# Polysketch attention with a multiplicative feed-forward block: first queries transferred behind the first keys, and a new order of all steps

## The chip, the cores and the metric

The kernel runs on one core of a Trainium2 chip. Its engines run side by side, each through its own row of instructions: TensorE (PE, with its weight loads listed as PEld), VectorE (DVE), ScalarE (ACT), GpSimd (POOL) and SyncE (SP), which here only issues transfers. The metric is the device time of one execution in microseconds (us), a median of several.

## The reference

There are 4 batches of 4 heads, 1088 positions a head and 32 numbers a position. Both sketches have 8 rows, so that a position has 64 features.

```python
def phi(x):
    a = np.einsum('rd,bhsd->bhsr', S1, x)
    b = np.einsum('rd,bhsd->bhsr', S2, x)
    return np.einsum('bhsi,bhsj->bhsij', a, b).reshape(*x.shape[:-1], r * r)
q_p, k_p = phi(q), phi(k)
kv = np.einsum('bhsf,bhsd->bhfd', k_p, v)
z = np.sum(k_p, axis=2)
num = np.einsum('bhsf,bhfd->bhsd', q_p, kv)
den = np.einsum('bhsf,bhf->bhs', q_p, z)[..., None] + 1e-06
attn = (num / den).astype(np.float32)
x = attn.transpose(0, 2, 1, 3).reshape(B * S, H * D)      # 4352 x 128
a, b = x @ w1, x @ w2                                     # 4352 x 1024
return ((a * b @ w3) @ w_out).astype(np.float32)          # 4352 x 128
```

## The kernel before

**What is computed.** The product w3 @ w_out is formed once (steps `f0` to `f7`), so that the feed-forward block is (x @ w1) * (x @ w2) times one 1024x128 matrix. Its 4352 rows of x are cut into eight groups of 512, `g0` to `g7`, two for each batch, and one of 256, `gr`, for the last 64 positions of each head. A group has eight parts of 128 columns. Part 3 of group 1, for example, has the steps `g1.3a` (x @ w1, L1799), `g1.3c` (a copy out of PSUM, L1804), `g1.3b` (x @ w2, L1809), `g1.3m` (the product on DVE, L1815) and `g1.3o` (the product with the folded matrix, L1835). Groups 4 and 5, and 6 and 7, are done together in a scheme with fewer multiplications, `h4` and `h6` (function `seven`): its products use only 64 rows of TensorE each. Products named `a` use rows 0 to 63 and those named `b` use rows 64 to 127 (L1673; a step such as `h4.0a5` is product 5 of part 0 in the lower half, with the tile `xd`), so that two of them can run at once; the later products, `P1` to `P7` (L1759), use 64 of the 128 columns, again a lower and an upper half.

**How x comes about.** For each batch the keys' steps are `k0` to `k3`: the keys are split in a leading part and a rest (`lead`, `rest`, L211), TensorE sums their outer products (`gram`, L659), several small steps turn these sums into scale factors (`k0.N0`, `k0.Na`, `k0.Nb` at L936 and L937, `k0.Nf` at L949 on POOL, which makes the tile `RS`), and the features meet the values (`kv`). The queries' steps are `q0`, `q1`, ..., one for each group at first: their sketches (`A`, `C`; `q0.C1` at L1030 multiplies the queries by `RS`), features (`phi`, L1208), denominators, and at last x, transposed (`q0.xT0`, `q0.xT1`, L1291). The first matmul of the feed-forward block, `g0.4a`, needs that x and columns of w1, which are converted from the raw words (`w1.c0`, `w1.j0` at L466, `w1.a0` on POOL at L470).

**What sets the order.** Every step is a small function under its name. The kernel calls 1179 steps in the order of a table, `ORDER`, and then ties the instructions of each engine into one row in that order, so that no engine takes a later instruction of its row before an earlier one has been issued. Further tables say which engine runs a step (`POOL` for GpSimd instead of VectorE, `CPV` for copies on VectorE instead of ScalarE) and which buffer each allocation takes (`SLOTS`; the tag `x`, with three buffers, holds q, k by heads and v). A buffer taken again makes its new writer wait for the last reader of its old content.

**Transfers.** Nearly all loads are issued by SP; the first two halves of the keys (`k0.load0`, `k0.load1`) are issued by ACT. A bulk load on SP also waits until the bulk load four places earlier has landed (`UNDER_WAY = 4`):

```python
for ins, ahead in zip(bulk[UNDER_WAY:], bulk):
    tc.add_manual_dep(ins, ahead.name, landed, reason="under way")
```

**Fillers.** Twelve steps `warm0` to `warm11` multiply a tile of zeros (L255, 128x256 each) on TensorE at chosen places; `WARM` says how many matmuls each has, in all 53.

Of the kernel before, what the change touches and what calls it, by code (L numbers as in the profile page):

```python
# [41 lines left out]
    "raw": "010212120211221",
    "s": "012345671252360063202461521024214",
    "x": "012012201110",
# [21 lines left out]
    g0.0c g0.1c h4.1ac h4.1ad h6.1bc h6.2ad k0.kT1 k1.kvc k2.kT1 k2.kq k3.kT0 k3.kT1 k3.kq q0.xc0  # L66
    q0.xc1 q6.xT0 q6.xT2
# [8 lines left out]
c.zeros warm0 q0.load c.ident s.four c.act c.mask s.zero k0.zero v0.zero s.load k0.load0 k0.loadr q0.restT q0.tr  # L76
k0.load1 s.words kr0.load k0.tr1 s.pair s.low s.lead s.sum k0.max0 k0.max1 warm1 q0.max k0.tr0 warm2 kr0.tr kr0.kT
warm3 s.rest w1.load s.T s.P s.tc warm4 q0.l2 k0.kT1 s.Pc s.R k0.g k0.lead0 s.c s.blk k0.rest0 q1.tr k0.gram0 s.blkh
k1.zero s.Pm warm5 q0.l1 q0.A0 warm6 kr0.ab k0.lead1 q0.rm q0.sma q0.sta warm7 k0.kT0 v0.load v0.loadr k1.load k0.ab1
q0.sha k0.rest1 q0.C0 k0.gram1 k0.gram2 k0.gram3 k0.gram4 k0.ab0 k0.abc1 q1.max q0.C0t q0.sla q1.l2 k1.loadr s.Pp  # L80
k0.Gm k0.Gt k0.Ga w1.c1 k0.Gb k0.abc0 k0.T0 q1.l1 warm8 kr0.abc k0.kp1 q0.sca w1.j1 k0.Ta k0.kp0 k0.Gc w1.c0 k1.tr0
kr1.load k2.zero k1.tr1 k1.kT1 kr0.kp warm9 k0.N0 warm10 k0.Na warm11 k0.T1 k0.kv0 k0.Tc k0.Tb k0.N1 k0.Nb k0.Nh q1.rm
q0.al k0.Nf q0.phi0 q0.phi1 q0.A1 q0.smy w1.m1 k1.max q0.sty q0.shy k0.kv3 k0.kv1 k0.kv2 q0.sly s.KS k0.kvr kr1.tr
# [1851 lines left out]
```

## Time and profile before

| | |
|---|---|
| device time, median of 3 runs | 245.06 us (244.8 to 246.78) |
| profiled execution, span from first to last instruction | 244.1 us |
| profiled execution, its own time | not listed beside its span |
| TensorE busy | 236.2 us (97%) |
| VectorE busy | 206.7 us (85%) |
| GpSimd busy | 161.9 us (66%) |
| ScalarE busy | 123.5 us (51%) |
| chain that ended last | 87% TensorE, 5% DMA |
| granted TensorE clock | 9 or more tenths in all 40 slices |

"Busy" is the time in which at least one instruction of an engine runs. The chain that ended last is followed back from the last instruction, at each step to whatever released it. The median stands 0.96 us above the profiled span; what lies around the span (launch and end) is in that difference.

### The profile page before, as it was taken

The page shows a single profiled execution, that of the slowest core. Times are in us where ns is not written, and L with a number is a line of the kernel's source. Part 1 is how long each engine was busy: PE and PEld are TensorE (multiplying, and loading weights), DVE is VectorE, ACT ScalarE, POOL GpSimd, SP SyncE. Part 2 cuts the span into 40 slices and gives each one's busy share as a digit, 9 for nine tenths or more (in the row PEclk, how much of TensorE's full clock was granted, in tenths as well). Part 3 has the DMA queues.
Part 4 walks back from the last instruction along what each step waited for, and adds up shares of the span by engine and source line. Part 5 has one row for each costly group of instructions (what it writes and reads, how often), then busy time and mean ns, then how long its engine had stood idle before and what let it go on. Part 6 is the DMA issues. An engine that isn't in the chain of part 4 may idle for free.

```text
span 244.1 us, 6745 instructions
## 1 busy us (share of the span) xinstructions
PE 236.2 (97%) x2724; PEld 129.8 (53%) x2724; DVE 206.7 (85%) x421; ACT 123.5 (51%) x246; POOL 161.9 (66%) x203
## 2 busy tenths in 40 slices
PE   8998999899999999999999999999999999999994
PEld 5887454545545646766566444444443354463363
DVE  2876988999899998997899878498989789999792
ACT  3976957675666764593012914355651164730010
POOL 4576658344856998764583889929999425883670
PEclk9999999999999999999999999999999999999999
DMA  7959797078859897200000000360000000000054
GB/s 201 265 143 325 181 227 190 6 197 224 220 141 251 188 217 190 59 1 3 3 0 0 4 0 3 59 113 3 1 0 0 0 3 0 0 1 3 12 90 93
DMA packets 31935, 22.06 MB, mean 90 GB/s; under 512 B 21280, under 2 KB 26528, under 8 KB 31904
## 3 DMA queue, kind: packets, MB, share of 16 engines
q1 hardware_dynamic: 31360, 21.11, 35.1%
q8 instruction: 21, 0.34, 0.6%
q10 hardware_dynamic: 544, 0.52, 0.6%
q14 instruction: 10, 0.08, 0.1%
HBM read 19.40 MB, written 2.23 MB: 89 GB/s over the span
## 4 chain that ended last, share of the span: by engine, by line
PE 87%; DMA 5%; ACT 2%; POOL 2%; DVE 1%; issue 1%; POOLq 0%; SPq 0%
PE b_ps L1809 12%; PE ps_o L1835 12%; PE ps_X L1673 11%; PE a_ps L1799 11%; PE ps_o L1759 10%; PE ps_w3o L534 6%; PE ps_Y L1673 6%; PE ps_Z L1673 3%; PE ps_g L659 2%; PE ps_x L1527 2%; PE ps_ac L1374 2%; DMA qh<-in_q_dram 2%; DMA k<-in_k_dram 2%; PE ps_or L1824 2%; POOL ph L1208 1%; PE idle_ps L255 1%
## 5 line engine op out<-in xcount | busy, mean ns | idle before, releaser
L1673 PE MATMUL ps_X<-xd,wv 64*128 64x512 f32 x112 | 36.3, 593 | 0.0
L1799 PE MATMUL a_ps<-xT,w 128*128 128x512 f32 (+1 forms) x80 | 36.1, 562 | 0.0
L1809 PE MATMUL b_ps<-xT,w 128*128 128x512 f32 (+1 forms) x80 | 35.6, 555 | 0.0
L1804 ACT COPY ffa<-a_ps 128x512 f32<-128x512 f32 (+1 forms) x38 | 20.1, 540 | 29.2 <-PE a_ps L1799 26.7
L1707 POOL TENSOR_TENSOR hc<-hc 128x512 f32<-128x512 f32 x16 | 20.7, 1304 | 15.7 <-DVE hc L1685 15.5
L1835 PE MATMUL ps_o<-ab,w3o 128*128 128x512 f32 x64 | 29.6, 600 | 0.0
L1680 ACT COPY hc<-ps_X 128x512 f32<-128x512 f32 x38 | 21.3, 590 | 16.1 <-PE ps_X L1673 12.9
L1815 DVE TENSOR_TENSOR ab<-ffa,b_ps 128x512 f32<-128x512 f32 (+1 forms) x40 | 23.9, 623 | 4.9 <-PE b_ps L1809 4.1
L501 POOL TENSOR_TENSOR w3c<-w3c,cv_m 128x512 int32<-128x512 int32 x16 | 21.2, 1344 | 4.2 <-DVE w3c L495 4.1
L1673 PEld LDWEIGHTS ps_X<-xd,wv 64*128 64x128 f32 x112 | 14.9, 186 | 13.1 <-issue 10.9
L1799 PEld LDWEIGHTS a_ps<-xT,w 128*128 128x128 f32 x80 | 14.1, 189 | 13.9 <-issue 8.8
L1809 PEld LDWEIGHTS b_ps<-xT,w 128*128 128x128 f32 x80 | 14.4, 190 | 13.1 <-issue 8.1
L1673 PE MATMUL ps_Y<-xd,wv 64*128 64x512 f32 x48 | 19.7, 594 | 0.0
L1835 PEld LDWEIGHTS ps_o<-ab,w3o 128*128 128x128 f32 x64 | 11.6, 190 | 13.4 <-issue 13.0
L534 PEld LDWEIGHTS ps_w3o<-wo,w3T 128*128 128x128 f32 x128 | 15.3, 192 | 2.4 <-issue 2.4
L534 PE MATMUL ps_w3o<-wo,w3T 128*128 128x128 f32 x128 | 15.7, 276 | 0.0
L1759 PE MATMUL ps_o<-hc,w3o 128*64 128x512 f32 x32 | 15.1, 595 | 0.0
L1759 PE MATMUL ps_o<-tt,ws 128*64 128x512 f32 x32 | 13.7, 594 | 0.0
L1680 ACT COPY hc<-ps_Y 128x512 f32<-128x512 f32 x14 | 8.1, 592 | 9.7 <-PE ps_Y L1673 6.6
L263 ACT ACTIVATE cv_c<-raw 128x1024 f32<-128x1024 f32 (+1 forms) x13 | 13.0, 1014 | 0.0
L1540 ACT COPY xd<-ps_x 64x256 f32<-64x256 f32 x24 | 8.8, 367 | 7.2 <-PE ps_o L1835 6.8
L1497 POOL COPY nz<-nz 32x8 f32<-32x8 f32 x32 | 11.1, 347 | 1.4
(347 smaller groups left out, 593.0 us busy)
## 6 DMA issues: line engine op xcount, KB each, us to landing
raw<-in_moe_w_dram SPq DMA_DIRECT2D x32, 256.0 KB, 5.0
qh<-in_q_dram SPq DMA_DIRECT2D x4, 544.0 KB, 4.5
raw<-in_moe_w_dram SPq DMA_DIRECT2D x4, 512.0 KB, 5.8
out_dram<-oT SPq DMA_DIRECT2D x32, 64.0 KB, 2.0
k<-in_k_dram SPq DMA_DIRECT2D x3, 512.0 KB, 5.1
v<-in_v_dram SPq DMA_DIRECT2D x2, 512.0 KB, 6.1
kh<-in_k_dram SPq DMA_DIRECT2D x8, 128.0 KB, 3.6
raw<-in_moe_w_out_dram SPq DMA_DIRECT2D x4, 256.0 KB, 5.0
```

Of the source, the lines that this page charges most:

```text
L263: act.activation(dst, hi.bitcast(F32), ACT.Prelu, scale=2.0 ** -112, alpha=-2.0 ** 32)
L501: pool.tensor_tensor(d, d, x["m"][:, i * 512:(i + 1) * 512], ALU.add)
L534: pe.matmul(t["o"], w3T[ko][:, c], wo[:, c], start=c == 0, stop=c == NC - 1)
L1673: pe.matmul(x[bank], stat(j, u)[:, i * 128:(i + 1) * 128], rows(j, u), start=new, stop=True, tile_position=(u * 64, 0), skip_group_check=True)
L1680: cp(n(y))(x[k], x[bank])
L1707: on(f"h{g}.{i}m{k}").tensor_mul(both[0][k], both[0][k], both[1][k])
L1759: pe.matmul(acc_o[bank][half[0]:half[1]], w(i), x(i), start=n == 1, stop=n == (2 if j == 3 else 4), tile_position=(0, half[0]), skip_group ...
L1799: pe.matmul(x["a"][:, :w], w_of(0, c), xT[g][:, c0:c0 + w], start=True, stop=True)
L1804: cp(f"g{g}.{c}{su}c")(x["s"][:, :w], x["a"][:, :w])
L1809: pe.matmul(x["b"][:, :w], w_of(1, c), xT[g][:, c0:c0 + w], start=True, stop=True)
L1815: dve.tensor_mul(ab_sb[g, c][:, c0:c0 + w], x["s"][:, :w], x["b"][:, :w])
L1835: pe.matmul(o_ps[g], w3o[:, c], ab_sb[g, c], start=n == 1, stop=n == NC)
```

## The change

Only tables change: `ORDER`, `SLOTS`, `POOL` and `CPV`. The set of steps is the same, and so is each step's arithmetic. In the order of loads on SP, the first queries (`q0.load`) move behind the sketch matrices and the last keys of batch 0, and the values of batch 0 and the keys by heads of batch 2 (`kh2.load`) trade places with other loads. The dummy activation `c.act` moves from the start to the end. 36 steps go from GpSimd to VectorE, 40 from VectorE to GpSimd, 7 copies from VectorE to ScalarE and 19 copies from ScalarE to VectorE. Lines of the diff, long tables cut:

```diff
 SLOTS = {
...
-    "x": "012012201110",
+    "x": "012011210102",
 }
...
 POOL = set("""
-    g4.oS g5.oS g6.oS g7.oS h4.0T1 h4.0T2 h4.0T3 h4.0m12 h4.0m22 h4.1T2 h4.1m11 h4.1m12 h4.2m11
+    g4.oS g6.oS h4.0T1 h4.0T2 h4.0T3 h4.0T4 h4.0m11 h4.0m12 h4.0m22 h4.1T1 h4.1T3 h4.1m11 h4.1m22
...
 CPV = set("""
-    g0.0c g0.1c h4.1ac h4.1ad h6.1bc h6.2ad k0.kT1 k1.kvc k2.kT1 k2.kq k3.kT0 k3.kT1 k3.kq q0.xc0
-    q0.xc1 q6.xT0 q6.xT2
+    g0.1c g1.3c g2.0c g2.1c g2.4c g3.6c h4.0ac h4.0bc h4.0bd h4.1ac h4.1be h4.2ac h4.2ad h4.k1
+    h6.0ac h6.0ae h6.1ac h6.3ae h6.3ai h6.3be k0.kT1 k2.kq k3.kq q0.xc0 q4.xT1 q6.xT0
...
 ORDER = """
-c.zeros warm0 q0.load c.ident s.four c.act c.mask s.zero k0.zero v0.zero s.load k0.load0 k0.loadr q0.restT q0.tr
...
-g1.oT g2.6o h4.1a5 g3.oT h4.0b5 h4.0bd h4.0a1 h4.0ac g2.oT h4.s3 h4.0b1 o.S2 h4.0bc h4.1a1 h4.1ac h4.1b1 h4.0b2 h4.0a2
+c.ident k0.zero k0.load0 c.zeros s.load k0.load1 s.words warm2 c.mask k0.loadr s.pair warm0 k0.tr0 s.low warm5 s.zero
...
+qr.phi0 v.4 g1.4o warm8 q6.pT1 q6.x q6.xT2 q6.xT3 g3.6o g0.oT g3.4o qr.pT0 g1.oT g2.oT h4.s1 qr.x q6.xT0 h4.0b1 q6.xT1
+h4.0a1 g3.oT h4.0a5 g0.st h6.s1 qr.xT0 h4.1b1 h4.s2 h4.0a2 h4.0b5 h4.s4 h4.s3 h4.0ac h4.0bc h4.0a6 h4.1a1 h4.0ah
...
 """
```

On SP, the first loads before, from the start of its row (`qh` are the queries of batch 0, `s_raw` the sketch matrices, `kr` the last keys, `raw` words of a weight matrix, here w1):

```order
L975 DMA qh<-in_q_dram 128x1088
L287 DMA s_raw<-in_S_dram 8x32 x2
L572 DMA k<-in_k_dram 64x4x32
L609 DMA kr_161<-in_k_dram 64x4x32 x2
L430 DMA raw<-in_moe_w_dram 128x512 x2
L582 DMA v<-in_v_dram 128x4x256
L593 DMA v<-in_v_dram 64x4x32
L560 DMA k<-in_k_dram 128x4x256
```

And now (`kh` are the keys of batch 2 by heads, in four pieces):

```order
L287 DMA s_raw<-in_S_dram 8x32 x2
L572 DMA k<-in_k_dram 64x4x32
L975 DMA qh<-in_q_dram 128x1088
L609 DMA kr_189<-in_k_dram 64x4x32 x2
L609 DMA kr_198<-in_k_dram 64x4x32 x2
L430 DMA raw<-in_moe_w_dram 128x512 x2
L572 DMA k<-in_k_dram 64x4x32
L560 DMA k<-in_k_dram 128x4x256
L593 DMA v<-in_v_dram 64x4x32
L582 DMA v<-in_v_dram 128x4x256
L601 DMA kh<-in_k_dram 32x1024 x4
```

The queries now stand behind three small loads. The values of batch 0 (`v`) stand behind the keys of batch 1, and take the buffer in which the queries of batch 0 were; `kh` has come forward, right behind them.

On DVE, the rows ahead of and with the first x before, from the sum `s_loy` of the step `q0.sly` on:

```order
L1101 TENSOR_TENSOR s_loy<-s_loy,ay_C_601 128x128
L1180 TENSOR_TENSOR s_pr<-s_al,s_loy 128x128
L1184 TENSOR_TENSOR s_pr<-s_pr 128x128
L1189 TENSOR_REDUCE s_d<-s_pr 128x2x16
L1194 SCALAR_TENSOR_TENSOR s_rc<-s_d 128x16
L1198 RECIPROCAL s_rc<-s_rc 128x16
L466 TENSOR_SCALAR w_81<-cv_c 128x2x256
L1274 COPY xc<-ps_xt 128x256 x2
L1291 TENSOR_TENSOR xT<-xc,ps_xs 128x256 x2
```

And now, between the same two steps (`s_hl`, `s_t_589` and `ay_C` of 128x384 belong to the queries of group 1, `kT` to the keys of batch 2):

```order
L1101 TENSOR_TENSOR s_loy<-s_loy,ay_C_574 128x128
L204 SCALAR_TENSOR_TENSOR s_hl<-s_g,s_t_589 128x2x128
L1157 TENSOR_TENSOR s_hl<-ps_a,s_hl 128x2x128
L1130 STREAM_TRANSPOSE ay_C<-ps_c 128x384
L1189 TENSOR_REDUCE s_d<-s_pr 128x2x16
L1194 SCALAR_TENSOR_TENSOR s_rc<-s_d 128x16
L1198 RECIPROCAL s_rc<-s_rc 128x16
L466 TENSOR_SCALAR w_81<-cv_c 128x2x256
L720 STREAM_TRANSPOSE kT<-kh 128x512
L1274 COPY xc<-ps_xt 128x256
L1291 TENSOR_TENSOR xT<-xc,ps_xs 128x256 x2
```

Two small products have gone to GpSimd and one copy to ScalarE; three steps of group 1 and the transposition of `kh` have come in between.

On TensorE, near the middle of its row, between the eighth-part products of the groups 0 to 3 (`ps_o`) and the products that make x of later groups (`ps_x`), there stands before:

```order
L534 MATMUL ps_w3o<-wo,w3T 128x128 x8
L1835 MATMUL ps_o<-ab,w3o 128x512
L1527 MATMUL ps_x<-pT,kq_2311 32x256 x32
L1835 MATMUL ps_o<-ab,w3o 128x512 x12
L1527 MATMUL ps_x<-pT,kq_2079 32x256 x32
```

And now:

```order
L1527 MATMUL ps_x<-pT,kq_2286 32x256 x32
L1835 MATMUL ps_o<-ab,w3o 128x512 x6
L255 LDWEIGHTS zeros
L255 MATMUL idle_ps<-zeros 128x256
L255 LDWEIGHTS zeros
L255 MATMUL idle_ps<-zeros 128x256
L1835 MATMUL ps_o<-ab,w3o 128x512
L255 LDWEIGHTS zeros
L255 MATMUL idle_ps<-zeros 128x256
L1527 MATMUL ps_x<-pT,kq_2328 32x256 x32
```

Three fillers (`warm7` and `warm8`) stand there now. Six more (`warm6`, `warm9`, `warm10`, `warm11`) have come from the start to places between these and the first feed-forward matmul.

163 lines of the change are left out of this document (81 added, 82 removed).

## The prediction

> **What bounds the kernel now.** I read the page's totals first, then the engines' busy time by stretches, with cuts at the first feed-forward matmul, at the ends of the regions without idle time, and at TensorE's last matmul.
>
> ```profile
> span 244.1 us, 6745 instructions
> PE 236.2 (97%) x2724; PEld 129.8 (53%) x2724; DVE 206.7 (85%) x421; ACT 123.5 (51%) x246; POOL 161.9 (66%) x203
> PE 87%; DMA 5%; ACT 2%; POOL 2%; DVE 1%; issue 1%; POOLq 0%; SPq 0%
> ```
>
> ```profile
> core 0: us, PE busy (x) PEld busy (x) DVE busy (x) ACT busy (x) POOL busy (x), PEclk, DMA share, GB/s
> 0.00:27.42 27.42, 24.49 (x506) 19.60 (x507) 18.01 (x58) 19.16 (x46) 15.23 (x52) 1.00 0.76 222
> 27.42:60.00 32.58, 31.18 (x625) 16.64 (x626) 29.44 (x81) 22.72 (x41) 17.94 (x24) 1.00 0.69 174
> 60.00:130.00 70.00, 70.00 (x941) 41.74 (x941) 63.71 (x124) 36.78 (x66) 52.19 (x42) 1.00 0.46 114
> 130.00:155.70 25.70, 25.70 (x255) 12.22 (x253) 20.19 (x39) 11.78 (x31) 19.60 (x20) 1.00 0.01 2
> 155.70:195.40 39.70, 39.70 (x185) 16.88 (x184) 34.25 (x55) 17.68 (x32) 30.78 (x34) 1.00 0.16 27
> 195.40:240.56 45.16, 45.16 (x218) 22.75 (x218) 40.86 (x67) 15.35 (x31) 26.18 (x35) 1.00 0.13 21
> 240.56:244.10 3.54, 0.00 (x0) 0.00 (x0) 0.29 (x1) 0.00 (x0) 0.00 (x0) 0.87 0.33 74
> ```
>
> TensorE is the bound from 27.42 to 240.56: from 60 on it is busy all the time, and 27.42 to 60 has 32.58 - 31.18 = 1.40 us without it. So an engine that gets faster or slower there changes nothing until TensorE waits for it. The change can move three things: when the feed-forward matmuls begin, how much TensorE has to do after that, and where it waits. Before 27.42 TensorE is busy too, but much of that is fillers; there the end of a chain decides, which I followed back from the first feed-forward matmul:
>
> ```profile
> 7.67 0.19 ACT L207 ACTIVATION_READ_ACCUMULATOR k_abs<-k 128x1 f32 x1
> 10.25 0.82 ACT L211 ACTIVATE kk<-k,k_g 128x640 f32<-128x640 f32 x1
> 18.96 0.16 DVE L937 TENSOR_TENSOR RC<-RC,ps_Nr 128x8 f32<-128x8 f32 x1 [0.41 <-PE ps_Nr L912]
> 19.20 0.67 POOL L949 TENSOR_TENSOR RS<-RC,mask 128x64 f32<-128x64 f32 x1
> 22.52 0.40 PE L1030 MATMUL ps_cy<-q,RS 128*32 128x128 f32 x8
> 23.20 0.32 DVE L1068 STREAM_TRANSPOSE ay_C<-ps_cy 128x128 f32<-128x128 f32 x1 [1.38 <-PE ps_cy L1030]
> 26.48 0.79 DVE L1291 TENSOR_TENSOR xT<-xc,ps_xs 128x256 f32<-128x256 f32 x2
> 27.42 1.96 PE L1799 MATMUL a_ps<-xT,w 128*128 128x512 f32 x4
> ```
>
> The keys' maxima are there at 7.67 + 0.19 = 7.86, but the second half's leading part (`k0.lead1`, ACT) starts only at 10.25, behind steps of the queries. From there sums and scale factors lead to 18.96 + 0.16 = 19.12 (`k0.Nb`), and from that 8.30 us lead to the first matmul: `RS` on POOL, `q0.C1`, for which DVE idles 1.38, and then DVE without a pause.
>
> **The start, part one: the keys' chain.** With the queries behind the first keys, `k0.lead1` stands on ACT directly behind the maxima. It can start some 10.25 - 7.86 = 2.4 us earlier; other small copies ahead of it take back a part. I take 2.1, as an estimate, for everything up to `k0.Nb`. The lower end is 0.5: the same 16 DMA engines carry everything (0.76 busy up to 27.42), and queries that land later may hold up what then stands behind them. The upper end is 3.5, if the keys land earlier too. Nine fillers (two each of `warm10`, `warm11` and `warm7`, one each of `warm6`, `warm8` and `warm9`) leave the first 18 us. Their price is the pitch of a run of them:
>
> ```profile
> 16.99 0.27 PE L255 MATMUL idle_ps<-zeros 128*128 128x256 bf16 x1
> 17.36 0.61 PE L255 MATMUL idle_ps<-zeros 128*128 128x256 bf16 x4
> ```
>
> (0.61 - 0.27) / 3 = 0.11 us each, 1.0 for nine. Ahead of the first feed-forward matmul they mostly filled waits; I credit the chain with half, 0.5.
>
> **The start, part two: DVE from `k0.Nb` to the first x.** Here the new row of DVE holds more. Added are `k0.kp1` (from POOL), `q0.al`, five steps of group 1 (`q1.sm`, `q1.st`, `q1.sh`, `q1.sl`, `q1.Ct`) and `k2.kT0`; two products and a copy go. The prices:
>
> ```profile
> L677 DVE TENSOR_TENSOR kp<-kab 128x1024 f32<-128x1024 f32 x1 | 1.2, 1206 | 0.0
> L720 DVE STREAM_TRANSPOSE kT<-kh 128x512 f32<-128x512 f32 x4 | 2.8, 704 | 0.3 <-POOL s_bs L1204 0.3
> L1137 DVE TENSOR_REDUCE s_g<-ps_a 128x32 f32<-128x256 f32 x1 | 0.4, 416 | 0.0
> L201 DVE SCALAR_TENSOR_TENSOR s_t<-s_g,ps_a 128x256 f32<-128x256 f32 x1 | 0.4, 420 | 0.0
> L204 DVE SCALAR_TENSOR_TENSOR s_hl<-s_g,s_t 128x256 f32<-128x256 f32 x3 | 1.3, 419 | 0.1
> L1157 DVE TENSOR_TENSOR s_hl<-ps_a,s_hl 128x256 f32<-128x256 f32 x1 | 0.4, 424 | 0.0
> L1130 DVE STREAM_TRANSPOSE ay_C<-ps_c 128x384 f32<-128x384 f32 x1 | 0.6, 575 | 0.0
> L1180 DVE TENSOR_TENSOR s_pr<-s_al,s_loy 128x128 f32<-128x128 f32 x1 | 0.3, 294 | 0.0
> L1274 DVE COPY xc<-ps_xt 128x256 f32<-128x256 f32 x2 | 0.7, 412 | 0.0
> ```
>
> 1.21 for `kp1`, 0.70 for `kT0`, 0.42 + 0.42 + 0.42 + 0.42 + 0.58 = 2.26 for group 1, and 0.28 for `al`, an estimate from the 128x128 product, add up to 4.45; away go `q0.p2` and `q0.p12` (0.29 each, the second of the same shape) and one copy (0.41): 1.0. That is 3.4 us more on DVE (one of two equal halves of `phi` comes and the other leaves). Against it stands the 1.38 of idle time, which the added work fills, since `kp1` needs nothing that comes late. The two products on POOL cost 0.3 more in handing over, an estimate from the gap of 0.08 before `RS` on each of four handovers. The start comes to -2.1 - 0.5 + 3.4 - 1.4 + 0.3 = **-0.3**, that is the first feed-forward matmul at about 27.1. Its range goes from -2.4 (all the new work in waits) to +2.5 (below).
>
> **TensorE after the start.** The useful work is the same. The nine fillers now stand where TensorE has no idle time: **+1.0**, and 0 if each falls into a wait.
>
> The products of `h4` and `h6` use half of the array, and two that use different halves run together:
>
> ```profile
> 156.67 0.59 PE L1673 MATMUL ps_X<-xd,w 64*128 64x512 f32 x1
> 156.68 0.59 PE L1673 MATMUL ps_X<-xd,wv 64*128 64x512 f32 x1
> 157.10 0.59 PE L1673 MATMUL ps_X<-xd,w 64*128 64x512 f32 x1
> 157.11 0.59 PE L1673 MATMUL ps_X<-xd,wv 64*128 64x512 f32 x1
> ```
>
> Each pass of a pair takes 157.10 - 156.67 = 0.43 us, and each product has two passes, so one that runs alone wastes 0.86 / 2 = 0.43. Of the 168 products, lower and upper ones alternated in pairs before. Now the order is `h4.0b1`, `h4.0a1`, `h4.0a5`, `h4.1b1`, `h4.0a2`, `h4.0b5`, and so on: between two instructions that use the whole array, I count 45 of one half and 44 of the other, then 25 and 26, then 14 and 14. Where TensorE lets a product of the free half go ahead, only the two odd ones run alone: **+0.9**, or 1.7 where its look-ahead is two products. It does go out of order elsewhere in the trace: the sums of the keys alternate two operands (`kk` and `k,kk`) head by head in the program, and still
>
> ```profile
> 9.50 0.33 PE L659 MATMUL ps_g<-kk 128*32 128x64 f32 x7
> 9.61 0.19 PE L659 MATMUL ps_g<-k,kk 128*32 128x32 f32 x1
> ```
>
> seven of one kind started ahead of the first of the other. [...]
>
> **Stalls from 27.42 to 60.** The largest piece of the 1.40 is
>
> ```profile
> 45.83 1.16 issue
> ```
>
> in the middle of the keys of batch 2 (the chain between 44 and 48 us). `k2.gram` now comes earlier among more matmuls of group 0, since the `kh` of batch 2 has come forward. I take half of the 1.40, **-0.7**; all of it may go (-1.4), and new waits of the same size may come (+1.2).
>
> POOL receives 24 us of DVE work and gives up 45 us; both engines stay below TensorE in every stretch after 60, where DVE has 70.00 - 63.71 = 6.3 us to spare and POOL 18. The copies moved between ACT and DVE are covered likewise; their cover is that TensorE has other parts' matmuls to do, and if it is gone the cost is a stall of one copy, about 0.6 us. The dummy activation at the end costs nothing: ACT is idle in the last stretch. The last 3.54 us are unchanged.
>
> **The sum.** Against the span of 244.1: -0.3 + 1.0 + 0.9 - 0.7 = +0.9, so 245.0. The median of the runs, 245.06, stands 0.96 above that span, which I take to be what lies around it: 245.0 + 0.96 = 246.0 us.
>
> **The rivals.** One per cent, about what a measurement of this kernel can tell from no change, lies at 242.6 and 247.5.
>
> *A, strict order of the halves.* If products start only in the order of the program, two neighbours of the same half cannot run together. Counting the order that way leaves 20 products alone: 20 x 0.43 = 8.6 instead of 0.9, or 246.0 + 7.7 = 253.7. For it speaks nothing in the rows, against it 9.50 and 9.61. 7%.
>
> *B, the late transfer.* The values of batch 0 now take the queries' buffer, so their load waits for `q0.restT` on DVE, which now stands behind the first sum of the keys; and the fourth piece of `kh` waits until those values have landed. `k2.kT0` needs all four pieces and stands on DVE ahead of the first x.
>
> ```profile
> v<-in_v_dram SPq DMA_DIRECT2D x2, 512.0 KB, 6.1
> kh<-in_k_dram SPq DMA_DIRECT2D x8, 128.0 KB, 3.6
> ```
>
> ```profile
> 14.91 0.19 DVE L217 TENSOR_REDUCE G_g<-ps_g 128x1 f32<-128x32 f32 x1 [1.35 <-PE ps_g L659]
> ```
>
> With `q0.restT` at about 13 (an estimate: the sum of `gram4` is taken up at 14.9 before, less 2.1), the last piece lands at 13 + 6.1 + 3.6 = 22.7, some 2 us ahead of DVE, which comes to it at about 25. If these loads take 2 us longer than that, for want of bandwidth, DVE stands still with all of group 0 behind it. At 4.5 us longer the first matmul is 2.5 late instead of 0.3 early: 246.0 + 2.8 = 248.8, slower. It decides from a landing of `kh` after 25 on. 16%.
>
> *C, the start gains in full.* The work added on DVE lies in waits, the first matmul comes 2.4 earlier (2.1 more than I took), the stalls go entirely (0.7 more) and the fillers stand in waits (1.0 less): 246.0 - 3.8 = 242.2, faster. For it speaks that most of the added DVE steps belong to group 1 and have to be done soon after anyway; against it that DVE had one pause only, of 1.38. 20%.
>
> *D, no gain on the keys' chain.* The loads share their engines, so the maxima or the sums come later by about 1.1 than I took: 247.1, within 1%. The change would then not do what its order of loads says. 10%.
>
> **How the numbers follow.** The forecast, 246.0, has the remaining 47%; D is within 1% as well: 0.57. Faster is C, 0.20. Slower are A and B, 0.23. The range runs from 242.0, just below C, to 249.0, just above B; outside lie A and the tails of B and C, less than 2 in 10. Each unknown's bounds alone stay in it: the start -2.4 to +2.5 gives 243.9 to 248.8, the stalls 245.3 to 247.9, the halves 246.0 to 246.8.
>
> **What would show it.** In the profile of the changed kernel: the first row of L1799 at about 27.1 (24.9 for C, 29.9 for B, with a wait of DVE at L720 released by the transfer `kh`); `k0.Nb` at about 17.0; passes of L1673 still in pairs 0.43 apart in the stretch of `h4` (single passes 0.43 apart there for A); nine fillers at L255 after the first L1799; less than 1.4 us without TensorE between its first L1799 and 60. It would be wrong as a whole if TensorE were idle for more than 2 us anywhere after 60: then a move of work between DVE, POOL and ACT, which I cost at nothing, would be the bound.

## The result and the profile after

The changed kernel takes 252.86 us (median of 4 runs, 252.56 to 254.27), beside 245.92 (244.8 to 246.78) for the kernel before: a ratio of 1.031, 95% interval 1.026 to 1.037. It is slower; 246.0 was forecast. Here and below a median is over all executions of a kernel, while ratios and intervals leave out those more than 1.5% above its fastest. The profiled span went from 244.1 to 250.8 us.

The page of the changed kernel, its totals, its chain by engine and its clock:

```profile
span 250.8 us, 6757 instructions
PE 243.6 (97%) x2724; PEld 143.2 (57%) x2724; DVE 216.3 (86%) x429; ACT 116.7 (47%) x234; POOL 147.0 (59%) x207
PE 86%; DVE 8%; DMA 2%; SPq 2%; issue 1%; ACT 0%; DVEq 0%
PEclk9957999999999999999999999999999999999999
```

TensorE has the same 2724 matmuls and is busy 243.6 - 236.2 = 7.4 us longer with them. In the third and fourth slice of the clock row (12.5 to 25 us) it ran at 0.5 and 0.7. The busy times by stretches, with cuts at the same events as before (first feed-forward matmul, first product of `h4`, TensorE's last matmul):

```profile
core 0: us, PE busy (x) PEld busy (x) DVE busy (x) ACT busy (x) POOL busy (x), PEclk, DMA share, GB/s
0.00:30.86 30.86, 27.69 (x497) 22.93 (x498) 19.63 (x63) 20.78 (x47) 16.17 (x54) 0.83 0.70 205
30.86:60.00 29.14, 29.04 (x606) 15.45 (x606) 28.45 (x72) 22.63 (x40) 11.10 (x20) 1.00 0.85 217
...
158.20:199.20 41.00, 41.00 (x184) 22.21 (x178) 35.90 (x57) 14.86 (x33) 31.31 (x34) 1.00 0.08 14
199.20:246.84 47.64, 47.63 (x224) 27.78 (x222) 42.86 (x72) 14.41 (x30) 25.91 (x43) 1.00 0.11 18
246.84:250.80 3.96, 0.00 (x1) 0.00 (x0) 0.11 (x1) 0.27 (x1) 0.00 (x0) 0.96 0.39 83
```

After the start TensorE is idle for 29.14 - 29.04 = 0.10 us and then never, and still the last two working stretches take 88.64 us where they took 84.85. The accounts, from the cuts of the two traces:

| stretch | before | after | difference |
|---|---|---|---|
| start to first feed-forward matmul | 27.42 | 30.86 | +3.44 |
| from there to the first product of `h4` | 128.29 | 127.34 | -0.95 |
| from there to TensorE's last matmul | 84.85 | 88.64 | +3.79 |
| tail | 3.54 | 3.96 | +0.42 |
| span | 244.1 | 250.8 | +6.7 |

So two places lose, the start and the products on half of the array. The start of the changed kernel, in order of time (start, length, then the wait before in brackets):

```profile
8.25 0.30 PE L819 MATMUL ps_krt<-ident,kr 128*128 128x128 f32 x1 [0.49 <-DMA kr<-in_k_dram]
11.01 0.30 PE L819 MATMUL ps_krt<-ident,kr 128*128 128x128 f32 x1 [0.72 <-DMA kr<-in_k_dram]
13.01 0.19 DVE L217 TENSOR_REDUCE G_g<-ps_g 128x1 f32<-128x32 f32 x1 [1.35 <-PE ps_g L659]
21.30 0.16 DVE L937 TENSOR_TENSOR RC<-RC,ps_Nr 128x8 f32<-128x8 f32 x1
29.03 0.70 DVE L720 STREAM_TRANSPOSE kT<-kh 128x512 f32<-128x512 f32 x1
30.86 1.10 PE L1799 MATMUL a_ps<-xT,w 128*128 128x512 f32 x2 [0.31 <-DVE xT L1291]
```

`k0.Gm` is taken up at 13.01 instead of 14.91, 1.90 earlier, as the order of loads promised. But `k0.Nb` ends at 21.30 + 0.16 = 21.46 instead of 19.12, 2.34 later, so that 8.45 us lie between the two where 4.21 did. From there to the first matmul it is 9.40 instead of 8.30, +1.10. The two rows of TensorE (`kr0.tr`, `kr1.tr`) wait for the last keys of batch 0; fillers stood about there before.

### The profile page after: what moved, and what is told of

Its sections match the earlier page's. It is cut to its first block, busy times and chain, and to the rows that moved or that the text cites. A ratio compares the mean times of both kernels' runs of the same rounds, so it can differ in the third digit from the quotient of the medians.

```text
span 250.8 us, 6757 instructions
## 1 busy us (share of the span) xinstructions
PE 243.6 (97%) x2724; PEld 143.2 (57%) x2724; DVE 216.3 (86%) x429; ACT 116.7 (47%) x234; POOL 147.0 (59%) x207
## 4 chain that ended last, share of the span: by engine, by line
PE 86%; DVE 8%; DMA 2%; SPq 2%; issue 1%; ACT 0%; DVEq 0%
PE ps_X L1673 12%; PE b_ps L1809 12%; PE ps_o L1835 11%; PE a_ps L1799 11%; PE ps_o L1759 10%; PE ps_Y L1673 6%; PE ps_w3o L534 6%; PE ps_Z L1673 3%; DMA kr<-in_k_dram 2%; PE ps_x L1527 2%; PE ps_ac L1374 2%; PE ps_g L659 2%; PE ps_or L1824 2%; PE ps_ab L702 1%; PE ps_kv L769 1%; DVE kk L651 1%
## 5 line engine op out<-in xcount | busy, mean ns | idle before, releaser
L1673 PE MATMUL ps_X<-xd,wv 64*128 64x512 f32 x112 | 41.4, 596 | 0.0
L1804 ACT COPY ffa<-a_ps 128x512 f32<-128x512 f32 (+1 forms) x34 | 17.4, 534 | 40.6 <-PE a_ps L1799 38.0
L501 POOL TENSOR_TENSOR w3c<-w3c,cv_m 128x512 int32<-128x512 int32 x16 | 22.2, 1404 | 6.1 <-DVE w3c L495 6.0
L1680 ACT COPY hc<-ps_X 128x512 f32<-128x512 f32 x29 | 15.9, 591 | 16.2 <-PE ps_X L1673 11.1
L1673 PEld LDWEIGHTS ps_X<-xd,wv 64*128 64x128 f32 x112 | 17.6, 186 | 9.2 <-issue 5.8
L1809 PEld LDWEIGHTS b_ps<-xT,w 128*128 128x128 f32 x80 | 14.3, 190 | 12.5 <-issue 9.0
L1673 PE MATMUL ps_Y<-xd,wv 64*128 64x512 f32 x48 | 21.1, 596 | 0.0
L1707 POOL TENSOR_TENSOR hc<-hc 128x512 f32<-128x512 f32 x14 | 17.7, 1269 | 2.5 <-DVE hc L1685 2.4
L1540 ACT COPY xd<-ps_x 64x256 f32<-64x256 f32 x24 | 8.8, 366 | 13.6 <-PE ps_x L1527 13.2
L1759 PE MATMUL ps_o<-hc,ws 128*64 128x512 f32 x32 | 14.6, 594 | 0.0
L538 ACT COPY w3o<-ps_w3o 128x128 f32<-128x128 f32 x8 | 2.1, 267 | 20.9 <-PE ps_w3o L534 20.9
```

The lines of the kernel that those rows point to most:

```text
L501: pool.tensor_tensor(d, d, x["m"][:, i * 512:(i + 1) * 512], ALU.add)
L1673: pe.matmul(x[bank], stat(j, u)[:, i * 128:(i + 1) * 128], rows(j, u), start=new, stop=True, tile_position=(u * 64, 0), skip_group_check=True)
L1680: cp(n(y))(x[k], x[bank])
L1707: on(f"h{g}.{i}m{k}").tensor_mul(both[0][k], both[0][k], both[1][k])
L1759: pe.matmul(acc_o[bank][half[0]:half[1]], w(i), x(i), start=n == 1, stop=n == (2 if j == 3 else 4), tile_position=(0, half[0]), skip_group ...
L1804: cp(f"g{g}.{c}{su}c")(x["s"][:, :w], x["a"][:, :w])
```

## Experiments on the start

**Nine fillers back at the start (changed kernel).** The first theory was that TensorE's waits, no longer filled, had brought its clock down.

```diff
-... warm1 kr0.tr kr0.kT ... s.blk kr1.tr ...          (warm6 to warm11 after 60 us)
+... warm1 warm6 warm7 warm8 kr0.tr kr0.kT ... s.blk warm9 warm10 warm11 kr1.tr ...
```

> The changed kernel, but the nine fillers that it had put behind the first feed-forward matmul stand at its start again: four ahead of kr0.tr and five ahead of kr1.tr, where its TensorE waited. Theory CLOCK (the granted clock fell to 0.50 from 11.7 to 21.6 us because TensorE was too idle between 7.3 and 10.9): the clock stays at 1.00, the first feed-forward matmul comes at 27 to 28.5 instead of 30.86, and with 1.0 us of late fillers gone the time falls by 3.5 to 5 us, to about 248.5. Rival ORDER (the wide sums of the keys ahead of k0.T0 on TensorE, and more steps on DVE, make the start late): the first feed-forward matmul stays above 30 and only the 1.0 us goes, about 251.8.

Measured: 249.90 us (249.52 to 250.44), 1.018 of the kernel before [1.014, 1.021], so 2.96 of the 6.9 us came back. The clock stayed at 1.00, `k0.Nb` ended at 19.34 and the first matmul began at 28.73 instead of 30.86. Stretches of the changed kernel:

```profile
7.00:11.00 4.00, 2.80 (x84) 2.21 (x83) 3.72 (x8) 3.29 (x9) 0.89 (x4) 1.00 0.84 217
11.00:14.00 3.00, 2.99 (x86) 2.82 (x87) 1.65 (x7) 2.07 (x6) 1.56 (x6) 0.59 0.78 249
14.00:17.00 3.00, 3.00 (x19) 2.99 (x18) 1.33 (x6) 2.07 (x5) 1.58 (x1) 0.50 0.54 141
```

and of the one with the fillers back:

```profile
7.00:11.00 4.00, 3.78 (x90) 2.70 (x89) 3.41 (x8) 3.18 (x11) 0.71 (x4) 1.00 0.82 212
11.00:14.00 3.00, 2.94 (x95) 2.53 (x94) 1.99 (x7) 2.90 (x6) 1.94 (x7) 1.00 0.80 251
14.00:17.00 3.00, 2.05 (x41) 1.85 (x40) 1.67 (x8) 2.21 (x6) 2.15 (x2) 1.00 0.62 136
17.00:20.00 3.00, 3.00 (x71) 2.58 (x62) 2.50 (x12) 2.75 (x8) 1.86 (x4) 1.00 0.71 227
```

With 2.80 of 4.00 us busy the clock fell to 0.59 and 0.50 behind it; with 3.78 it did not. Four more profiles have this same start in the orders below: first matmuls at 28.75, 29.23 and 28.97 where the clock held, and at 31.28 where it fell.

The clock is not the whole difference between the two kernels. The four executions of the changed kernel took 252.56 and 252.90 us at a mean clock of 0.979 and 0.977, and 252.82 and 254.27 at 0.993: those that lost less clock were not shorter.

**The late fillers taken out altogether (changed kernel).**

```diff
-WARM = [27, 2, 3, 4, 4, 4, 1, 2, 1, 1, 2, 2]
+WARM = [27, 2, 3, 4, 4, 4, 0, 0, 0, 0, 0, 0]
```

> The changed kernel without the nine late fillers. CLOCK and ORDER both say that the start is unchanged (first feed-forward matmul at 30.9, clock 0.50 from 11.7 to 21.6); the fillers stood where TensorE had no idle time, so 1.0 us goes: 251.8. If they stood in waits, nothing goes: 252.8.

Measured: 251.76 us (251.45 to 252.04), 1.025 [1.022, 1.028], 1.1 less than the changed kernel. Not all of this is the nine fillers' own time. From the first feed-forward matmul to `h4`, idle time taken off, the changed kernel takes 127.34 - 0.10 = 127.24 us, this one 126.63, and three of the runs with the fillers at the start 126.4 to 126.7: they cost 0.6 to 0.9 there. In this run's start stands a wait that the changed kernel has not:

```profile
15.90 0.66 PE L702 MATMUL ps_ab<-RS,kT 128*128 128x64 f32 x5 [2.11 <-issue]
```

and behind it the clock fell to 0.50 too, but for 3.41 us only, where the changed kernel had 10.24; the first matmul came at 29.95. So the clock is not all that makes the start late; what the wait put down to "issue" is comes out two experiments on.

**The second wait for the last keys moved back (changed kernel).**

```diff
-... s.blk kr1.tr q0.l2 ... k0.N1 kr0.kp ...
+... s.blk q0.l2 ... k0.N1 kr1.tr kr0.kp ...
```

> The changed kernel with kr1.tr, which waited on TensorE until 10.88 for its transfer, behind k0.N1. CLOCK: the idle time of 0.7 us ahead of it becomes some 0.3, and the clock either holds (first feed-forward matmul at 27 to 28.5, time about 249.5) or falls all the same because of the idle time between 7.3 and 9. ORDER: about 0.3 us earlier, 252.5.

Measured: 252.29 us, 1.027 [1.023, 1.031], no gain that counts. The wait of 0.72 was gone (one of 0.49 for DVE took a part of its place) and TensorE was busy 3.31 of the 4 us from 7 to 11; but a wait of 1.99 us at 15.81, again put down to "issue", followed, and the clock was at 0.50 from 17 to 20. It is not that one wait which decides. The clock fell under the new wait, at 15.39; up to there it had held.

**The same nine fillers taken from the kernel before.** The edit is that of `WARM` above.

> The kernel before without its last nine fillers (warm6 to warm11), which stand between 10 and 18 us. CLOCK: TensorE is less busy there, and if that is what holds the clock, it falls below 1.00 in the first 25 us and the first feed-forward matmul comes 1 to 3 us later than 27.4: 246.5 to 248.5. Rival: they only filled waits, the clock stays at 1.00, and the time is 245 to 245.9.

Measured: 251.03 us (250.36 to 251.36), 1.022 [1.018, 1.025], 5.6 us more. That is far more than the fillers' share in the changed kernel, and its profile shows another cause ahead of the clock:

```profile
24.30 0.87 PE L769 MATMUL ps_kv<-kp,v 128*32 128x64 f32 x24 [4.45 <-issue]
24.00:26.00 2.00, 1.70 (x41) 1.29 (x45) 0.00 (x0) 0.55 (x3) 0.00 (x0) 0.50 0.05 14
```

For 4.45 us TensorE waited for nothing that the profile shows, in the middle of `k0.kv`. The kernel before has two such rows in its own trace, at a matching place and at the stall that the prediction halved:

```profile
20.35 0.69 PE L769 MATMUL ps_kv<-kp,v 128*32 128x64 f32 x34 [0.91 <-issue]
46.98 0.19 PE L659 MATMUL ps_g<-k,kk 128*32 128x32 f32 x1 [1.16 <-issue]
```

Counted along TensorE's row, weight loads included, all these waits stand at its instruction 449, 705 or 1729, that is 193 plus 1, 2 and 6 times 256. The page has a queue for it, the same in both kernels (packets, MB, share):

```profile
q8 instruction: 21, 0.34, 0.6%
```

21 packets for 0.34 MB are 16 KB each, and 2724 matmuls with as many weight loads are 21.3 times 256: about one packet for 256 instructions of TensorE, an estimate from these counts. In the run above such a packet went from 22.0 to 22.9, and TensorE went on at 24.30; in the kernel before it ended at 18.94 and TensorE went on at 20.35. So I take these waits, of 0.91 to 4.45 us, to be for the next block of instructions. Why a packet comes late, here at 22.0, no run was made to show.

**Named part of the change alone (kernel before).** The queries' load behind the first keys, with the keys' steps and sums moved forward as the change has them, and nothing else:

```diff
-c.zeros warm0 q0.load c.ident ... k0.loadr q0.restT q0.tr k0.load1 ... kr0.tr kr0.kT ... q0.A0 ... kr0.ab k0.lead1 ...
+c.zeros warm0 c.ident ... k0.loadr q0.load k0.load1 ... kr0.tr k0.g k0.lead0 k0.lead1 kr0.kT ... k0.gram4 k0.Gm k0.Gt k0.Ga q0.A0 ...
```

> The kernel before with only the edit that names the change: q0.load behind k0.loadr on SP, and with it k0.g, k0.lead0, k0.lead1, k0.rest0, k0.rest1, k0.gram1 to k0.gram4 and k0.Gm to k0.Ga ahead of the first steps of the queries on their engines. Theory KEYS: k0.Gm starts 1.9 us earlier, as it did in the changed kernel (13.0 instead of 14.9), and a part of it, 0.5 to 1.5, reaches the first feed-forward matmul: 244 to 244.9. Rival LOST: TensorE's steps behind it (k0.ab0, k0.T0, code that comes late, the clock) take it back, first feed-forward matmul at 27.4 or later: 245.4 or more.

Measured: 246.59 us (245.69 to 249.85, 8 runs), 1.006 [1.004, 1.008]. Its own rows:

```profile
13.19 0.19 DVE L217 TENSOR_REDUCE G_g<-ps_g 128x1 f32<-128x32 f32 x1 [1.72 <-PE ps_g L659]
20.66 0.16 DVE L937 TENSOR_TENSOR RC<-RC,ps_Nr 128x8 f32<-128x8 f32 x1 [0.41 <-PE ps_Nr L912]
27.92 1.10 PE L1799 MATMUL a_ps<-xT,w 128*128 128x512 f32 x2
```

The same as in the changed kernel, with all fillers at the start: `k0.Gm` 1.7 earlier, `k0.Nb` 1.7 later, the first matmul 0.5 later. What the loads give the keys is taken back between `k0.Gm` and `k0.Nb`. The rows say where: ahead of `k0.T0` (L883), the first product of TensorE behind `k0.Gm`. First the kernel before, then the changed kernel with the nine fillers back:

```profile
15.81 0.25 PE L883 MATMUL ps_T<-RS,G_a 128*32 128x32 f32 x2
```

```profile
15.30 1.08 PE L702 MATMUL ps_ab<-RS,kT 128*128 128x64 f32 x8
16.32 0.22 PE L883 MATMUL ps_T<-RS,G_a 128*32 128x32 f32 x1
```

From `k0.Gm` to `k0.T0` it is 15.81 - 14.91 = 0.90 us in the first and 16.32 - 13.02 = 3.30 in the second (3.64 in the run with the named part); from there to the end of `k0.Nb` it is 3.31 and 3.02. The kernel before did the wide sum `k0.ab0` (L702, about 1 us) at 11.07, when the second half of the keys had not yet been split, and `kr0.ab` and `q0.A0` ahead of the keys' last sums too; only the second wide sum, `k0.ab1`, stood before `k0.T0`. With the keys there first, all of these stand behind the keys' last sum, from 12.91 on, and a wait of 0.95 us for a block of instructions falls among them. That block set a floor of its own: in the run without late fillers `k0.Gm` came as early as 11.97, and `k0.T0` at 16.50, behind the wait of 2.11 us.

**Keys' steps ahead of the queries' (nine fillers back at the start).** If the wide sums that stand between (`k0.ab1`, `q0.C0`) hold up the chain on TensorE, taking the chain first should free it.

```diff
-kr0.ab q0.A0 k0.ab1 k0.abc0 ... k0.Ta q0.C0 k0.abc1 ... k0.N0 ... k0.Nb ... k0.Nf
+kr0.ab k0.abc0 ... k0.Ta q0.A0 k0.ab1 ... kr0.abc k0.T1 k0.Tb k0.Tc k0.N0 k0.abc1 q0.C0 k0.Na k0.N1 k0.Nh k0.Nb k0.Nf
```

> early_fill, with k0.T0 on TensorE ahead of q0.A0 and k0.ab1, and k0.T1, k0.N0 and k0.N1 ahead of k1.tr1 and mostly of q0.C0; the steps of DVE, ACT and POOL that answer to them move along. Theory TE-ORDER (the gain of 1.9 us at k0.Gm is lost again up to k0.Nb because TensorE does wide sums first): k0.Nb ends at about 17.8 instead of 19.3, and as DVE has no idle time from there on, the first feed-forward matmul comes at about 27.4 instead of 28.7: 248.6. Rival: DVE or ACT were in the way as well, k0.Nb ends at 19 or later, and nothing is won.

Measured: 253.52 us, 1.034 [1.029, 1.038]. `k0.Nb` ended at 19.37, no earlier than 19.34, and what had been moved back came too late (second row):

```profile
15.10 0.25 PE L883 MATMUL ps_T<-RS,G_a 128*32 128x32 f32 x2 [1.24 <-DVE G_b L865]
25.43 0.88 PE L769 MATMUL ps_kv<-kp,v 128*32 128x64 f32 x48 [1.41 <-DVE kp L677]
```

The first part of the chain was freed, though: `k0.T0` began at 15.10 instead of 16.32, directly behind a wait of 1.24 us, which is for a block of instructions (it stands at TensorE's instruction 449) and not for DVE, as the row has it. The gain was lost again at the end, where DVE waited 1.35 us for `k0.N1`, which now stood behind `q0.C0` on TensorE, while the clock was at 0.50 (0.58 as a mean from 17 to 20 us). So what stands on TensorE between that wait and `k0.T0` does hold the chain, by 1.2 us; this order as a whole is no better, and it is no clean test of what the chain could gain.

**DVE unloaded ahead of the first x (nine fillers back at the start).**

```diff
-q0.pt0 q1.Ct ... q0.pt1 q1.sca ... w1.j0 q1.p01 ... q0.x1 k2.kT0 ... q0.xT0 q1.al ... q1.scy k1.ab k2.load ... g0.4a
+q0.pt0 ... q0.pt1 ... w1.j0 ... q0.x1 ... q0.xT0 q1.Ct k2.kT0 q1.sca q1.p01 q1.al ... q1.scy k2.load ... g0.4a k1.ab
```

> early_fill, with q1.Ct and k2.kT0 (with q1.sca and q1.p01 on POOL) behind q0.xT0 on their engines, and k1.ab behind g0.4a on TensorE. Theory DVE-ROW (DVE is without a pause from k0.Nb to the first x, so each step added there delays the start by its whole time): 0.5 + 0.5 us less, first feed-forward matmul at 27.7 instead of 28.7, time 249.0. Rival: another engine is as late (w1 on POOL), and less than 0.3 is won.

Measured: 252.52 us (250.75 to 256.11), 1.027 [1.021, 1.032]; the first matmul at 31.17. As a test of DVE's row it is inconclusive, since the clock fell in its profiled execution; its two executions with a mean clock of 0.997 took 250.75 and 252.36, no less than 249.90, so nothing speaks for a gain. But it settles another thing. Up to 24 us its order is that of the first experiment, and so are TensorE's waits, yet:

```profile
14.00:17.00 3.00, 2.06 (x20) 1.93 (x21) 2.22 (x10) 2.35 (x7) 1.68 (x2) 0.95 0.17 28
17.00:20.00 3.00, 3.00 (x39) 2.75 (x39) 1.48 (x8) 1.43 (x5) 1.27 (x3) 0.50 0.91 289
```

With 2.06 us busy of 3.00 the clock went to 0.50, with 2.05 in the first experiment it stayed at 1.00. In these runs the clock changed in steps of 3.41 us, as the last section shows: here the gap of 0.94 us lies inside one step (13.31 to 16.73, 2.48 us busy), in the first experiment, where the clock did not change, the like gap of 0.95 lies, by the count of the steps, across the end of one at 14.83 (2.82 us busy before it, 3.05 behind). That this is the reason is not shown. `k0.Gm` to `k0.Nb` took 6.32 us with the clock held and 7.83 with it halved: **1.5 us for the clock alone**. The gap is a wait for a block of instructions as well. Two runs with this start below, whose clock held, took 5.7 (a wait of 0.32 there) and 5.5 (none), because `k0.Gm` came later in them; `k0.Nb` ended at 19.83 and 19.35.

## Experiments on the products of half the array

For a run of half-array passes I take half of 0.43, the pitch of a pair in the kernel before, as the least time: 0.214 us a pass, if both halves are always taken; what the run takes beyond that, from the start of its first pass to the start of its last, I call lost. In three runs without whole-array work between, the kernel before loses 0.09, -0.09 and 0.05 us, the changed one 2.53, 0.79 and 0.90, in all 4.2. One group of products on the page, first of the kernel before, then of the changed one (busy us, mean ns of one, idle before):

```profile
L1673 PE MATMUL ps_X<-xd,wv 64*128 64x512 f32 x112 | 36.3, 593 | 0.0
```

```profile
L1673 PE MATMUL ps_X<-xd,wv 64*128 64x512 f32 x112 | 41.4, 596 | 0.0
```

The same 112 passes, each as long as before, spread over 5.1 us more, and no idle time at all: fewer of them run beside another.

**Halves paired in the table (nine fillers back at the start).** 19 products pulled forward so that lower and upper ones alternate again, such as:

```diff
-... h4.0a6 h4.1a1 h4.0ah h4.0ad h4.0ae h4.0b6 ...
+... h4.0a6 h4.0b6 h4.1a1 h4.0ah h4.0ad h4.0ae ...
```

> early_fill (249.9), with 19 of the half-array products taken forward, so that lower and upper ones alternate in pairs again but for 5; no other instruction moves. Lost lanes in early_fill against two products in 0.86 us: 2.5 in the run from h4 on, 0.8 in the next, 0.9 in the last, 4.2 us in all. Theory LOOK-AHEAD (TensorE lets a product of the free half go ahead past at most one further pending product of the other half, three passes in all): only the odd ones stay, 0.4 + 0.4 + 0, and what was lost to the order, 0.9, comes back: about 249; the rest, 2.5, is waits for other engines. Theory PAIRS (the losses are the order's doing altogether): 3.3 comes back, about 246.6. If products started only in the order of the program, the losses would have been 8.6 already.

Measured: 250.46 us, 1.021 [1.017, 1.025], no better than 249.90, and lost are 2.47, 0.85 and 0.90. The order of the halves in the table is not the cause, which both theories put to this run had held.

**Runs of one half put into the kernel before.** The other way round: its later products `P` ordered so that three to six of one half follow each other in places.

```diff
-... h4.0P6 h4.3ai ... h4.1P4 ... h4.0P4 ... h4.1P7 ...
+... h4.1P4 h4.0P4 h4.1P7 h4.0P6 ...
```

> The kernel before, with the products P1, P2 and P4 to P7 of h4 and h6 put in runs of up to four of the same half, as far as their inputs allow. Lost lanes in the run of h4 and in that of h6, counted for each depth: strict order 4.3 and 3.4; two passes pending on a half 2.6 and 1.3; three 1.7 and 0; four 1.3 and 0; six 0.4 and 0. LOOK-AHEAD as read from the changed kernel says three: 1.7 and 0, time about 247.

Measured: 247.33 us in one run, beside 245.17; lost are 1.87, -0.09 and 0.22. A model of a TensorE that keeps up to three passes of each half pending loses 1.7 and 0 in the first and the third, one that starts strictly in the program's order 4.3 and 3.4; in the second, where the halves alternate, both lose nothing. So rival A's mechanism is refuted in numbers, and the order does cost something where runs of one half are put in: 1.87 us in the first run of passes, where the kernel before lost 0.09. In the changed kernel that is not what costs, since pairing brought nothing.

What the lost passes wait for is seen one by one. With the nine fillers back, the first product passes of `h4`:

```profile
155.49 0.69 PE L1673 MATMUL ps_X<-xd,wv 64*128 64x512 f32 x1
155.99 0.69 PE L1673 MATMUL ps_X<-xd,w 64*128 64x512 f32 x1
156.95 1.02 PE L1673 MATMUL ps_Y<-xd,wv 64*128 64x512 f32 x2
157.52 0.69 PE L1673 MATMUL ps_X<-xd,wv 64*128 64x512 f32 x1
```

They come half a microsecond and more apart. The pass at 155.99 was released by a copy of `xd` on ACT (L1540) at 155.94, that at 157.52 by the next at 157.48. TensorE counts as busy all the time, with one half (in the changed kernel for 41.00 of 41.00 us from 158.20 on). Later, in the same kernel:

```profile
170.44 1.29 POOL L1727 TENSOR_TENSOR tt<-hc 128x512 f32<-128x512 f32 x1
170.49 1.79 DVE L1707 TENSOR_TENSOR hc<-hc 128x512 f32<-128x512 f32 x1
172.20 0.68 DVE L1712 TENSOR_TENSOR hc<-hc,ps_X 128x512 f32<-128x512 f32 x1
172.93 0.18 PEld L1673 LDWEIGHTS ps_Z<-xd,wv 64*128 64x128 f32 x1 [0.52 <-DVE hc L1712]
```

Here the later half stands until a product of DVE has emptied its PSUM bank at 172.20 + 0.68 = 172.88; DVE is late because its instruction before took 1.79 instead of 0.68 us, beside one of POOL. Of that more below.

**Two copies of x given to DVE (nine fillers back at the start).** Two of the copies of `xd` go from ACT to DVE:

```diff
 CPV = set("""
+    q6.xT1 q6.xT2
```

> early_fill, with two of the three copies that put x of groups 6 and 7 together and that ran on ACT (q6.xT1 and q6.xT2) on DVE. In early_fill the first products of h4 start 0.04 us after a copy of ACT (L1540 at 155.94 and 157.48, L1549 at 157.78), and 0.8 us of lanes is lost there. Theory COPIES (the lanes are lost because operands and PSUM buffers come free late): this 0.8 shrinks to 0.4 or less, time 249.4 or less. Rival (order of the products): the 0.8 stays, 249.9.

Measured: 257.06 us (253.22 to 257.65), 1.041 [1.032, 1.050]. The profile is of the shortest execution, 253.22, whose clock held; the other three, at a mean clock of 0.986 and 0.987, took 256.74 to 257.65. So in this execution the copies themselves cost 253.22 - 249.90 = 3.3 us. It is the wrong way to the right place (its lines are one higher):

```profile
158.75 0.69 PE L1674 MATMUL ps_X<-xd,wv 64*128 64x512 f32 x1 [0.79 <-DVE xd L1541]
161.35 0.66 PE L1674 MATMUL ps_Y<-xd,wv 64*128 64x512 f32 x1 [1.40 <-DVE oT L1843]
```

DVE now comes late with the copies and with what stands behind them, by more than ACT did; lost in the first run of passes are 2.63. So single copies do set this stretch, but giving two of them to DVE costs more than it gains.

**Engine sets exchanged.** The tables `POOL` and `CPV` of `h4` and `h6` of each kernel put under the order of the other (the changed one with the nine fillers back):

```diff
 POOL, CPV of the changed kernel:
-    the names h4.* and h6.* of the changed kernel
+    those of the kernel before
```

> early_fill, with the steps of h4 and h6 on the engines on which the kernel before has them; the order stays. Theory SETS (the lanes are lost because the changed engines are late with copies and sums): 4.2 us of lost lanes becomes 2 or less, time 247.7 to 248.5. Rival (the order of the steps, whatever the engines): lost lanes 3.5 or more, 249.5 or more.

```diff
 POOL, CPV of the kernel before:
-    the names h4.* and h6.* of the kernel before
+    those of the changed kernel
```

> The kernel before, with the steps of h4 and h6 on the engines on which the changed kernel has them; its order stays. SETS: lost lanes 2 to 4 us, 247.5 to 249. Rival (order): 0.5 or less, 245.2 to 245.9.

Measured: 258.37 us, 1.055 [1.051, 1.059], and 261.82 us, 1.068 [1.063, 1.072]. From the first product of `h4` to TensorE's end they take 96.19 and 100.10 us, where the two parents take 88.65 and 84.85. Neither set is the slow one. An order holds only with the engines for which it was made, and moves between engines, which the prediction costed at nothing, are worth 7.5 and 15 us where the order was not made for them.

**Sums shortened (nine fillers back at the start).** The last theory: TensorE's halves wait for single late sums and products of the other engines. This kernel leaves out most of that work: all these sums and products on 64 of 512 columns leave DVE and POOL free early.

```diff
-dve.tensor_add(x[k], x[k], x[bank])
+dve.tensor_add(x[k][:, :64], x[k][:, :64], x[bank][:, :64])      (likewise the products m11, m12, m22 and m21)
```

> early_fill, with the sums (L1685, L1712) and products (L1707, m21) of h4 and h6 on DVE and GpSimd done for 64 of the 512 columns only; this leaves a part of the computation out and takes some 0.5 us from each of 56 sums and 8 products on DVE and about 1 us from each on GpSimd. TensorE's instructions and every engine's order stay. Theory WAITS (the 4.2 us of lost lanes are waits of single products for sums and copies that come late): the lanes lost in the middle of the runs, where a sum of DVE is named (172.9, 178.2, 205, 215.1), go, and with them 1.5 to 2.5 us; the 0.8 at the beginning, which waits for copies of ACT that stay, is left: 247.5 to 248.5. Rival ORDER (the order of the halves on TensorE): 4.2 us stay, 249.6 to 250.2.

Measured: 248.56 us (247.99 to 249.2), 1.013 [1.008, 1.017], 1.3 less than with the sums whole. Lost are 1.17, 0.53 and 0.90, that is 1.6 less, and the single losses from 171 to 178 us are gone. The same place in it:

```profile
170.83 0.28 DVE L1707 TENSOR_TENSOR hc<-hc 128x64 f32<-128x64 f32 x1
171.43 0.22 DVE L1712 TENSOR_TENSOR hc<-hc,ps_X 128x64 f32<-128x64 f32 x1 [0.32 <-PE ps_X L1673]
```

DVE now waits for TensorE and no longer the other way. So 1.6 of the 4.2 us are waits for late sums and products. Some 0.8 at the start of `h4` are waits for the copies of x on ACT, as the rows above show but no run took away. Of the rest, 0.9 in the last run of passes and about 0.9 elsewhere (products without a partner, which the prediction counted at 0.9, may be part of it), the cause stays open.

## Why the prediction was wrong, point by point

| term | forecast | measured |
|---|---|---|
| keys' chain up to `k0.Nb`, with the early fillers | -2.1 - 0.5 | +2.34 |
| `k0.Nb` to the first matmul | +2.3 | +1.10 |
| fillers after the start | +1.0 | +0.6 to 0.9 |
| stalls up to 60 us | -0.7 | -1.30 |
| products of half the array | +0.9 | +4.2 |
| tail | 0 | +0.42 |

These make 7.4 to 7.7 of a measured 6.7; the rest, in the stretches between, was not followed up.

**The keys' chain** is the first step that failed, by 4.9 us. That `k0.Gm` would come about two microseconds earlier was right (1.90). Two things were wrong. The fillers were credited with a gain of 0.5, because they "mostly filled waits"; but filling waits was worth more than the waits. Without them the clock halved, which cost 1.5 us (7.83 against 6.32) in the pair of executions that differ by it alone. And the gain was carried on up to `k0.Nb` as if nothing else stood between. At full clock `k0.Gm` to `k0.Nb` takes 5.5 to 6.3 us instead of 4.21, and `k0.Nb` ends at 19.34 at the earliest, against 19.12, so that all of the 1.90 is gone even then: TensorE now does behind the keys' last sum what it did ahead of it before, and there the next block of instructions comes late (a wait of 0.95 us with the nine fillers back). The named part alone on the kernel before shows it too. This is what rival D says, with 10%, but not by D's mechanism: the keys' sums did not come later, the steps behind them did.

**DVE from `k0.Nb` on** was costed too high, by 1.2. The pause of 1.38 was filled, as forecast. But the added work lengthened the row by 9.40 - (8.30 - 1.38) = 2.5 instead of 3.4. In part this is because steps of group 1 now stand between steps that wait for one another: the next step stands 0.20, 0.19 and 0.20 us behind `s_gy`, `s_t` and `s_hiy`, where the dependent one stood 0.31, 0.33 and 0.55 behind. The 0.3 for handing over did not show. **B's** chain didn't happen: the fourth piece of `kh` landed at 21.19, and the transposition (L720, at 29.03) starts without a wait. **C** fell with the chain.

**The stalls** went nearly entirely, 1.30 of 1.40, but not by the place of `k2.gram`, from which the forecast took its half: the one of 1.16 was a wait for TensorE's next block of instructions. That packet now landed at 43.10, and TensorE came to the block at 46.98 without a wait; before, the packet ended at 45.43. That the sign was right is luck.

**The halves**: the count of single products was the wrong measure. TensorE did go out of order, as the rows of the keys' sums had suggested: the run with fours lost 1.87 and 0.22 us where a strict order, in the model above, would lose 4.3 and 3.4, and with that **A** is refuted. But the step that failed is the one after it: "both engines stay below TensorE in every stretch after 60", hence moves between DVE, POOL and ACT at nothing. A mean over 40 us says nothing of the one sum that the next product waits for. The test that I set for it, TensorE idle for more than 2 us, could not see it either: with one half at work TensorE counted as busy, for 41.00 of 41.00 us from 158.20 on.

**The tail** of +0.42 is a term that I left out. It lies in the row of SP. The last store is issued behind eight others, about 0.5 us each, and in the changed kernel these end at 245.93 + 1.60 = 247.53, after the last copy (247.15). In the kernel before they end at 230.45 + 10.14 = 240.59, ahead of the last copy's end (240.89), so that the copy set the time (rows of the kernel before, then of the changed one):

```profile
230.45 10.14 SPq L1556 DMA_DIRECT2D out_dram<-oT  x16
240.60 0.29 DVE L1858 COPY oT<-ps_or 128x128 f32<-128x128 f32 x1 [1.41 <-PE ps_or L1824]
240.95 0.62 SPq L1562 DMA_DIRECT2D out_dram<-oT  x1
```

```profile
245.93 1.60 SPq L1556 DMA_DIRECT2D out_dram<-oT  x3
246.88 0.27 ACT L1858 COPY oT<-ps_or 128x128 f32<-128x128 f32 x1 [2.87 <-PE ps_or L1824]
247.64 0.62 SPq L1562 DMA_DIRECT2D out_dram<-oT  x1
```

The last store is thus issued 247.64 - 246.84 = 0.80 us after TensorE's last matmul, where it was 0.39. That the last copy went from DVE to ACT is not the reason by these rows; no run tried it.

## What to carry to other kernels

A filler on TensorE is priced by what its absence does to everything behind it, to the clock and to the waits for blocks of instructions, not by the wait that it fills: count TensorE's busy share over every 3 to 4 us of a start. Here the clock fell behind 2.54 and 2.48 of 3.41 us, 74% and 73%; it is no rule, as the next section shows. At work on halves of its array, TensorE was 100% busy here (41.00 of 41.00 and 47.63 of 47.64 us) and lost 4.2 us in all; count passes times the pitch of a pair against the length of the run before calling other engines covered. Before an early gain is carried to the end of a chain, look which work used to run in the wait that is gone, and where in the chain it stands now.

## What the runs showed of the hardware

**The clock.** At these starts it stayed at 0.50 for 3.41 (`no_late_fill`), 6.83 (`kr1_later`) or 10.24 us (the changed kernel): once, twice and three times 3.41. In the traces of the two kernels it stayed at 1.00 for 238.93 us (before) and for 6.83 and 228.69 us (changed), 70, 2 and 67 times 3.413. It fell without any long wait: in the changed kernel after gaps of 0.49 and 0.72 us, at the end of a step of 3.41 us with 2.54 us busy (8.10 to 11.51), and elsewhere with 2.48 of 3.41 (`dve_unload`) and with 1.19 and 1.10 of 3.00 us (`kr1_later` and `no_late_fill`, 14 to 17 us). But the busy share alone does not decide: the clock held with 2.00 of 3.00 in `x_copies` and 2.01 in `short_sums` (26 to 29 us), and with 1.88 of 3.41 later in `x_copies` (153.18 to 156.59). What decides beside the share, these runs do not show.

**Blocks of instructions.** TensorE stood for up to 4.45 us (`before_less_fill`) where, by the count above, a block of 256 instructions ended and the next had not landed. In the kernel before it went on 1.33, 1.41 and 1.55 us after the end of the packet (packets to 12.94, 18.94 and 45.43, instructions 449, 705 and 1729 at 14.27, 20.35 and 46.98), in `before_less_fill` 1.4 (22.9 to 24.30). The profile calls such a wait "issue" (0.91, 1.16, 1.99, 2.11 and 4.45 us above) or names another engine (0.95 us ACT, 1.24 us DVE).

**DVE beside POOL.** A product of two tiles `hc` on DVE (L1707) took 1.79 us instead of 0.68, its median in the traces of both kernels, where POOL had begun a product of its own, of 1.29 us, 0.05 us earlier (the rows at 170.44 and 170.49 above). It ended 0.55 us after POOL's.
